# Three small loads moved to the large loads' queue, and the gates computed after q

## The chip, the core and the metric

The kernel runs on one core of one Trainium2 chip. The metric is the time of one execution on the device in microseconds (us). Before the change it was 1347.45 us, the median of three runs (1345.95 to 1347.85).

Engines are called PE (matmuls), PEld (weight loads of PE), DVE (VectorE), ACT (ScalarE), POOL (GpSimd) and SP (SyncE). A "q" behind the name is the engine's sequencer, which issues the transfers and waits on semaphores. A "packet" is one piece of a transfer on one of the core's 16 DMA engines, as the profile records it. A run is called fast here when it took at most 1.5% more than the fastest run of the same kernel.

## The reference

For four sequences of one token each, the kernel mixes an attention block over a cache of 8192 positions with a gated feed-forward block.

```python
g = sigmoid((x * gate_w).sum(-1, keepdims=True))
# a: attention. 4 sequences, 32 heads of 128, 8192 cached positions
q = (x @ wq).reshape(4, 1, 32, 128).transpose(0, 2, 1, 3)
p = softmax(q @ k_cache^T * 128 ** -0.5)
a = (p @ v_cache) ... @ wo
# b: feed-forward, scaled by sigmoid(x @ w_r), plus x   (one token: the argsort picks it)
b = x + ((silu(x @ w_gate) * (x @ w_up)) @ w_down) * sigmoid(x @ w_r)
return g * a + (1 - g) * b
```

Every weight and both caches are read once. The profile counts 575.68 MB of reads, and 93% of that is the two caches (2 x 4 x 32 x 8192 x 128 x 2 bytes = 536.9 MB).

## The kernel before

All large loads go through one ring of five slots in on-chip memory (`ring`, 4 MB each) and through SyncE's queue. A load waits until the slot it overwrites has been read. The first of them, `wq` (8 MB, slots 0 and 1), is hoisted to the very start of the program. A "pair" is 8 MB of the K or of the V cache, in two halves of one slot each. `w_gate` follows in slots 2 and 3, and the first half of K pair 0 in slot 4. The second half of K pair 0 goes into slot 0 again, so it waits for the q matmuls that read the half of `wq` in that slot.

```python
x6 = const.tile([NX, D], BF)             # 4 rows of x, then w_r, then gate_w
nc.scalar.dma_start(out=x6[0:Bn], in_=x2)
nc.scalar.dma_start(out=x6[Bn:Bn + 1], in_=B_w_r.rearrange("(o n) -> o n", o=1))
nc.scalar.dma_start(out=x6[Bn + 1:Bn + 2], in_=gate_w.rearrange("(o n) -> o n", o=1))
... # x6 is transposed on PE and copied to xw
def gates():
    rg_ps = small([P, 2, Bn])
    wrep = ttp.tile([P, 2, DT, P], BF, name="wrep", tag="T")
    for i in range(2):
        nc.vector.tensor_copy(out=wrep[:, i, :, :], in_=xw[:, :, Bn + i:Bn + i + 1].to_broadcast([P, DT, P]))
        for t in range(DT):
            nc.tensor.matmul(rg_ps[:, i, :], lhsT=wrep[:, i, t, :], rhs=xT[t], start=(t == 0), stop=(t == DT - 1))
    nc.scalar.activation(out=sgb[:], in_=rg_ps[:], func=ACT.Sigmoid)
    ...
def wq_piece():
    N = H * Dh
    ws = load_pair(A_wq.rearrange("(c t) n -> c (t n)", t=DT), TW * N)
    x_rows(q_ps, ws, N // NB, lambda w, t, i: w[:, t * N + i * NB:t * N + (i + 1) * NB])
...
gates()
wq_piece()
q_done()
gu_piece(B_w_gate, 0)
... # then 32 pairs of K and of V halves, with w_up, w_down and wo in between
```

PE, DVE and POOL run their instructions in the order of the program.

## Time and profile before

| what | where it is read | value |
|---|---|---|
| time | median of three runs | 1347.45 us |
| bytes moved | DMA part of the page | 576.2 MB, mean 429 GB/s |
| SyncE's queue (q1) | queues, share of 16 engines' span | 99.4% |
| PE, DVE busy | first part of the page | 78%, 46% |
| q matmuls | timeline | 27.1 to 32.9 us |
| first use of w_gate | timeline | 39.85 us |

The lines below are from the page of the kernel before: the busy shares in 40 slices of the span (tenths, 9 is 90% or more), the rate in each slice, the DMA queues (packets, MB, share of 16 engines' span) and the shares of the chain that ended last.

```profile
...
PE   2565877777887778778987789797779679877888
...
DVE  3555655534445554345555446246545254556000
...
DMA  9999999999999999999999999999999999999997
GB/s 414 447 421 428 441 426 428 442 435 422 435 436 426 440 417 431 443 429 434 435 433 431 433 425 431 435 431 438 431 420 438 435 426 432 430 426 438 426 425 327
...
q1 hardware_dynamic: 14120, 575.68, 99.4%
...
q10 hardware_dynamic: 20, 0.02, 0.0%
...
DMA 63%; PE 19%; DVE 11%; issue 7%; another core or an unknown queue 0%; DVEq 0%; ACT 0%; SPq 0%
...
```

The DMA row reads 9 in every slice but the last, and no engine's row does. The chain is mostly DMA too. Queue q10 is ScalarE's: 20 packets, 0.02 MB.

Next is the timeline of the first 62 us (start, duration, engine, line, operation, out<-in, in brackets the idle time before and what ended it). L157 transposes x, L219 is the gates' broadcast copy, L244 holds the matmuls of q (`S_ps`) and of w_gate (`o_ps`).

```profile
...
0.00 0.40 SPq L127 DMA_DIRECT2D ring<-in_A_wq_dram  x1
...
0.80 0.56 ACTq L140 DMA_DIRECT2D x<-in_A_x_dram  x1
...
0.81 0.33 SPq L127 DMA_DIRECT2D ring<-in_B_w_gate_dram  x1
...
1.19 29.92 SPq L131 DMA_DIRECT2D ring<-in_A_k_cache_dram  x2
...
20.20 0.63 PE L157 MATMUL small<-identb,x 6*128 6x6 bf16 x8 [20.20 <-DMA x<-in_gate_w_dram]
...
21.18 5.60 DVE L219 COPY wrep<-xw 128x1024 bf16<-128x1024 bf16 x2
...
27.14 5.73 PE L244 MATMUL S_ps<-ring,xw 128*4 128x512 bf16 x64
...
39.85 6.21 PE L244 MATMUL o_ps<-ring,xw 128*4 128x512 bf16 x56 [3.81 <-DMA ring<-in_B_w_gate_dram]
...
44.33 0.33 SPq L127 DMA_DIRECT2D ring<-in_A_k_cache_dram  x1
...
```

PE stands idle for x until 20.20 us, then waits for the gate copies, and q runs from 27.14 us. But even so it is done before w_gate is there: PE waits another 3.81 us for it.

The third view is SyncE's waits in the first 60 us (line, what for, us in total, times, longest).

```profile
...
SPq L131 <- DMA ring<-in_A_wq_dram: 21.3, 1, 21.3
...
SPq L131 <- PE S_ps L244: 7.9, 1, 7.9
...
```

SyncE waits for the q matmuls once, for 7.9 us, before it can issue the second half of K pair 0.

### The profile page before, as it was taken

What the parts mean: (1) busy time and instruction counts of PE and PEld (TensorE: products, weight loads), DVE (VectorE), ACT (ScalarE), POOL (GpSimd) and SP (SyncE); (2) the same over time, 40 slices, a digit from 0 to 9 for tenths busy, and PEclk for the clock granted to TensorE, in tenths of its full rate; (3) what the DMA queues carried; (4) which work ended last, traced back from release to release, by engine and by line L of the source; (5) the groups of instructions that cost most, each with busy time, mean ns of one, the idle gap of its engine ahead of it and who ended that gap; (6) DMA issues with size and microseconds to landing.
All of it is one profiled execution on the core that took longest, in us unless ns stands there. A gap on an engine that the chain in (4) does not pass through costs nothing.

```text
span 1344.6 us, 7989 instructions
## 1 busy us (share of the span) xinstructions
PE 1050.9 (78%) x4536; PEld 229.7 (17%) x2348; DVE 620.5 (46%) x358; ACT 51.4 (4%) x46; POOL 57.7 (4%) x91
## 2 busy tenths in 40 slices
PE   2565877777887778778987789797779679877888
PEld 0111111112111121111211121111111112111211
DVE  3555655534445554345555446246545254556000
ACT  0000100001000100001000010001000010000000
POOL 3000100001000100001000010000000010000000
PEclk9787988988998889899888889998889898989999
DMA  9999999999999999999999999999999999999997
GB/s 414 447 421 428 441 426 428 442 435 422 435 436 426 440 417 431 443 429 434 435 433 431 433 425 431 435 431 438 431 420 438 435 426 432 430 426 438 426 425 327
DMA packets 14175, 576.20 MB, mean 429 GB/s; under 512 B 1582, under 2 KB 1590, under 8 KB 2108
## 3 DMA queue, kind: packets, MB, share of 16 engines
q1 hardware_dynamic: 14120, 575.68, 99.4%
q8 instruction: 27, 0.44, 0.1%
q14 instruction: 8, 0.07, 0.0%
q10 hardware_dynamic: 20, 0.02, 0.0%
HBM read 575.68 MB, written 0.01 MB: 428 GB/s over the span
## 4 chain that ended last, share of the span: by engine, by line
DMA 63%; PE 19%; DVE 11%; issue 7%; another core or an unknown queue 0%; DVEq 0%; ACT 0%; SPq 0%
DMA ring<-in_A_k_cache_dram 52%; DVE T L370 11%; PE S_ps L376 11%; PE o_ps L447 8%; DMA ring<-in_A_v_cache_dram 7%; DMA ring<-in_B_w_gate_dram 3%; DMA ring<-in_A_wo_dram 1%; PE small L466 1%; DVEq L370 0%; PE acc L210 0%; ACT OS L459 0%; ACT res L513 0%; DVE rinv L420 0%; DVE OS L460 0%
## 5 line engine op out<-in xcount | busy, mean ns | idle before, releaser
L370 DVE STREAM_TRANSPOSE T<-ring 128x2048 uint32<-128x2048 uint32 x256 | 570.5, 2281 | 497.8 <-DMA ring<-in_A_k_cache_dram 416.6
L376 PE MATMUL S_ps<-T,Z 128*128 128x512 bf16 x2048 | 538.3, 411 | 222.3 <-DVE T L370 222.3
L447 PE MATMUL o_ps<-ring,PB 128*32 128x512 bf16 x2048 | 458.0, 386 | 33.4 <-DMA ring<-in_A_v_cache_dram 33.3
L376 PEld LDWEIGHTS <-Z 128*128 128x128 bf16 x1024 | 106.5, 104 | 646.8 <-issue 638.8
L447 PEld LDWEIGHTS <-PB 128*32 128x32 bf16 x1024 | 100.3, 98 | 388.1 <-issue 367.5
L401 ACT ACTIVATE PTs<-S_ps,negm 128x1024 bf16<-128x1024 f32 x8 | 8.9, 1114 | 994.8 <-DVE negm L398 994.8
L353 POOL TENSOR_TENSOR Z<-qa,mq 128x16 bf16<-128x16 bf16 x32 | 8.2, 260 | 809.3 <-PE S_ps L376 734.9
L460 DVE SCALAR_TENSOR_TENSOR OS<-o_ps,mE,OS 128x512 f32<-128x512 f32 x8 | 6.0, 751 | 66.8 <-ACT OS L459 66.8
L412 POOL COPY PB<-PT 32x1024 bf16<-32x1024 bf16 x16 | 30.3, 1892 | 26.8 <-DVE rex L414 26.5
L410 ACT COPY PB<-PT 32x1024 bf16<-32x1024 bf16 x16 | 30.6, 1913 | 10.7 <-DVE PT L403 10.6
L309 DVE CAST LT<-small 128x64 bf16<-128x64 f32 x2 | 0.5, 225 | 46.3 <-PE small L307 46.3
L394 POOL PARTITION_ALL_REDUCE gmx<-mex x8 | 3.2, 394 | 339.0 <-DVE mex L391 339.0
L389 DVE TENSOR_REDUCE m<-S_ps 128x1 f32<-128x1024 f32 x8 | 9.8, 1225 | 15.9 <-PE S_ps L376 15.9
L210 PE MATMUL acc<-ring,LT 128*4 128x512 bf16 x64 | 14.9, 378 | 2.0 <-DMA ring<-in_A_wo_dram 1.2
L157 PE MATMUL small<-identb,x 6*128 6x6 bf16 x8 | 0.6, 196 | 20.2 <-DMA x<-in_gate_w_dram 20.2
L420 DVE RECIPROCAL rinv<-tot 128x16 f32<-128x16 f32 x8 | 2.0, 247 | 31.0 <-POOL tot L416 31.0
L403 DVE STREAM_TRANSPOSE PT<-PTs 128x1024 bf16<-128x1024 bf16 x8 | 10.0, 1246 | 12.1 <-ACT PTs L401 12.1
L466 PEld LDWEIGHTS small<-selg,OS 128*128 128x128 f32 x64 | 12.7, 279 | 6.0 <-issue 5.5
L210 PE MATMUL acc<-ring,hT 128*4 128x512 bf16 x56 | 12.2, 379 | 0.0
L466 PE MATMUL small<-selg,OS 128*128 128x16 f32 x64 | 11.7, 320 | 0.0
L459 ACT ACTIVATE OS<-o_ps,mE 128x512 f32<-128x512 f32 x8 | 5.5, 687 | 118.3 <-PE o_ps L447 118.3
L244 PE MATMUL o_ps<-ring,xw 128*4 128x512 bf16 x56 | 6.2, 573 | 3.8 <-DMA ring<-in_B_w_gate_dram 3.8
(71 smaller groups left out, 88.2 us busy)
## 6 DMA issues: line engine op xcount, KB each, us to landing
ring<-in_A_k_cache_dram SPq DMA_DIRECT2D x14, 4096.0 KB, 33.4
ring<-in_A_v_cache_dram SPq DMA_DIRECT2D x14, 4096.0 KB, 29.6
ring<-in_B_w_gate_dram SPq DMA_DIRECT2D x1, 7168.0 KB, 39.0
ring<-in_B_w_up_dram SPq DMA_DIRECT2D x1, 7168.0 KB
ring<-in_B_w_down_dram SPq DMA_DIRECT2D x2, 3584.0 KB, 25.7
ring<-in_A_wo_dram SPq DMA_DIRECT2D x6, 1024.0 KB, 22.2
ring<-in_A_v_cache_dram SPq DMA_DIRECT2D x2, 2048.0 KB, 31.1
ring<-in_A_v_cache_dram SPq DMA_DIRECT2D x4, 1024.0 KB, 29.0
```

The lines of the kernel that those rows point to most:

```text
L210: nc.tensor.matmul(out_ap, lhsT=lhsT, rhs=rhs, start=start, stop=True, skip_group_check=True)
L244: nc.tensor.matmul(ps[32 * k:32 * k + Bn, z, :], lhsT=xT[TW * half + t], rhs=cols(w, t, 4 * z + k), start=(half + t == 0), stop=(half == 1 ...
L353: nc.gpsimd.tensor_tensor(out=Z[:, :, QP - 1:QP - 1 + P].rearrange("p e (q c) -> p e q c", c=QP)[:, :, :, 0], in0=qa[:, :, h0:h0 + NQ, b], ...
L370: nc.vector.transpose(out=T[:].rearrange("p j h i e -> p (j h i e)").bitcast(U32), in_=kn[:, c * CJ * Dh:(c + 1) * CJ * Dh].bitcast(U32))
L376: nc.tensor.matmul(sps[:, z, :], lhsT=Z[:, he, s:s + P], rhs=T[:, 16 * z:16 * z + 16, half, :, e], start=(t == 0 and n == 0 and he == 0), ...
L389: nc.vector.tensor_reduce(out=m1[:], in_=sps[:].rearrange("p z n -> p (z n)"), axis=AX.X, op=ALU.max)
L401: nc.scalar.activation(out=PTs[:], in_=sps[:].rearrange("p z n -> p (z n)"), func=ACT.Exp, bias=negm[:, 0:1], scale=scale, accum_out=rs[:, ...
L403: nc.vector.transpose(out=PT[:].rearrange("p j i -> p (j i)"), in_=PTs[:])
L410: nc.scalar.copy(out=Bv[at, :, :, q, :], in_=Pv[at])
L412: nc.gpsimd.tensor_copy(out=Bv[at, :, :, q, :], in_=Pv[at])
L447: nc.tensor.matmul(o_ps[row:row + NM, e, :], lhsT=B_[:, RD * t + c, z, w].rearrange("p e s j -> p (e s j)"), rhs=vn[:, j0 * Dh:(j0 + 4) * ...
L466: nc.tensor.matmul(oT[:, :], lhsT=o_sb[:, q * Dh:(q + 1) * Dh], rhs=selg[:, q].rearrange("p t s -> p (t s)"), start=(q == 0), stop=(q == 3))
```

## The change

The intent: the small loads shall stop competing as a second queue with `wq`, and q, which K pair 0's slot waits for, shall come before the gates, which nothing needs early.

```diff
+    N = H * Dh
+    wq_at = load_pair(A_wq.rearrange("(c t) n -> c (t n)", t=DT), DT // 2 * N)
     NX = Bn + 2
     x6 = const.tile([NX, D], BF)
-    nc.scalar.dma_start(out=x6[0:Bn], in_=x2)
-    nc.scalar.dma_start(out=x6[Bn:Bn + 1], in_=B_w_r.rearrange("(o n) -> o n", o=1))
-    nc.scalar.dma_start(out=x6[Bn + 1:Bn + 2], in_=gate_w.rearrange("(o n) -> o n", o=1))
+    nc.sync.dma_start(out=x6[0:Bn], in_=x2)
+    nc.sync.dma_start(out=x6[Bn:Bn + 1], in_=B_w_r.rearrange("(o n) -> o n", o=1))
+    nc.sync.dma_start(out=x6[Bn + 1:Bn + 2], in_=gate_w.rearrange("(o n) -> o n", o=1))
 ...
     def wq_piece():
-        N = H * Dh
-        ws = load_pair(A_wq.rearrange("(c t) n -> c (t n)", t=DT), TW * N)
-        x_rows(q_ps, ws, N // NB, ...)
+        x_rows(q_ps, wq_at, N // NB, ...)
 ...
-    gates()
     wq_piece()
     q_done()
+    gates()
     gu_piece(B_w_gate, 0)
```

More of the change, by code (lines that the diff above doesn't have):

```diff
@@ L247, in wq_piece @@
     def wq_piece():
-        N = H * Dh
-        ws = load_pair(A_wq.rearrange("(c t) n -> c (t n)", t=DT), TW * N)
-        x_rows(q_ps, ws, N // NB, lambda w, t, i: w[:, t * N + i * NB:t * N + (i + 1) * NB])
+        x_rows(q_ps, wq_at, N // NB, lambda w, t, i: w[:, t * N + i * NB:t * N + (i + 1) * NB])
     def q_done():
```

## The prediction

> **What bounds the kernel now.** The transfers. The page shows 576.2 MB at a mean of 429 GB/s; the SyncE queue (q1) is busy 99.4% of 16 engines' span, and every slice but the last reads 9 in the DMA row. PE is busy 78%, DVE 46%. The Trainium skill, page "DMA: Bandwidth & Descriptors", section "Where 436 GB/s comes from", gives 435 GB/s as the fabric's ceiling; the trace's 429 is 98.6% of it, so start, tail and all starved moments together can hardly hold more than 20 us. The tail shows in the timeline: about 6 us after the stream has ended at 1338 us. The change doesn't touch it.
>
> **What the change does.** (a) Three small loads (12 KB) go from ScalarE's queue to SyncE's, behind wq and ahead of w_gate. (b) The gates' two copies on DVE, 16 matmuls and sigmoid go from before the q matmuls to after q is done.
>
> Timeline of before: wq is issued at 0 us and lands at 22.9 us. The small loads, issued by 2.2 us, land only at 20.2 us: their separate queue gave no early arrival (so says the same page, "Issuing engines are not separate DMA queues"). The transposes of x end by 21.0 us, the gate copies run 21.2 to 26.8 us (slow, while GpSimd clears PB), the gate matmuls end at 27.2, the q matmuls run 27.1 to 32.9, q is done at 36.8. The w_gate matmuls wait for their transfer until 39.85 us.
>
> After: x6 lands between 20 and 24 us, q matmuls start at 23 to 25 us (limited by wq's landing) and end near 29 to 31, q is done near 33 to 35, the gates are over by 37. The q stage gains 2 to 4 us. Issuing the small loads on SyncE costs about 1.3 us (0.56, 0.24 and 0.50 us on ScalarE) and delays w_gate's issue from 0.8 to about 2.1 us, with 20 us of wq queued.
>
> **How much is on the critical path.** Almost nothing. The gain ends in the wait for w_gate at 39.85 us. The one issue that q releases is the second half of K pair 0 (31.1 us, after 7.9 us of waiting for the q matmuls); it moves to about 27 us. But by 31.1 us 19.9 MB had been issued and about 12.5 MB moved (estimate: 29 us at 429 GB/s): 17 us of transfers were queued. The next issues (44.3, 58.2, 89.8 us) are released by w_gate matmuls and K transposes, behind the stream; by the same estimate 14, 19 and 5 us were queued there. The queue doesn't run dry before or after.
>
> **Prediction.** 1346.5 us, range 1343 to 1350; faster by over 2%: 0.01, within 2%: 0.98, slower by over 2%: 0.01.
>
> **What would show it.** Right: DMA row 9 throughout at about 429 GB/s; q matmuls about 3 us earlier, gates between q done and w_gate, w_gate matmuls still starting at 39.5 to 40.5 us, K pair 1 still issued at 44 to 45 us, the same tail. In the waits, SyncE's wait for the q matmuls falls from 7.9 to about 4 us. Wrong: x6 landing past 25 us, w_gate's matmuls moving with it, or a slice of the DMA row under 9.
>
> **What would make it wrong.** Small packets in SyncE's rings holding up w_gate or K; a slot freed in another order so that the thin 5 us of queue near 90 us runs dry; a different mean transfer rate from run to run (0.3% is 4 us).

## The result, and the profile after

The changed kernel took 1344.95 us (median of four runs, 1344.77 to 1345.52), beside 1347.65 us of the kernel before (four runs, the three above and one more, 1345.95 to 1349.12). The ratio is 0.9981, with a 95% interval from 0.9964 to 0.9998. A ratio here is the mean time of one kernel's fast runs over that of the other's of the same rounds, so it isn't quite the ratio of the medians. So the change is within 2%, as forecast. The interval stops just short of 1, so the first question is whether the 2.7 us between the medians are real.

These are the same parts of the changed kernel's page.

```profile
...
DMA  9999999999999999999999999999999999999998
GB/s 414 440 427 431 436 430 425 446 427 424 440 430 427 440 433 422 442 434 428 436 434 433 424 431 436 434 434 439 418 424 437 434 429 434 432 429 442 422 425 335
...
q1 hardware_dynamic: 14132, 575.69, 99.5%
...
q10 hardware_dynamic: 8, 0.00, 0.0%
...
DMA 62%; PE 20%; DVE 11%; issue 6%; another core or an unknown queue 0%; DVEq 0%; ACT 0%; SPq 0%
...
```

The rows are those of before: 9 in every slice but the last, and the same rate within the spread of the slices. The 12 packets of the small loads have gone from q10 to q1; the 8 left on q10 are the output's.

This is its timeline (source lines are shifted by two: L159 transposes x, L221 is the gate copy, L246 holds the matmuls of q and w_gate).

```profile
...
0.00 0.39 SPq L127 DMA_DIRECT2D ring<-in_A_wq_dram  x1
...
0.80 0.34 SPq L142 DMA_DIRECT2D x<-in_A_x_dram  x1
...
1.75 0.36 SPq L127 DMA_DIRECT2D ring<-in_B_w_gate_dram  x1
2.15 24.79 SPq L131 DMA_DIRECT2D ring<-in_A_k_cache_dram  x2
...
22.35 0.62 PE L159 MATMUL small<-identb,x 6*128 6x6 bf16 x8 [22.35 <-DMA x<-in_gate_w_dram]
...
23.24 5.04 PE L246 MATMUL S_ps<-ring,xw 128*4 128x512 bf16 x64 [0.27 <-DVE xw L161]
...
32.00 1.35 DVE L221 COPY wrep<-xw 128x1024 bf16<-128x1024 bf16 x2
...
39.00 5.72 PE L246 MATMUL o_ps<-ring,xw 128*4 128x512 bf16 x56 [5.22 <-DMA ring<-in_B_w_gate_dram]
...
43.44 0.33 SPq L127 DMA_DIRECT2D ring<-in_A_k_cache_dram  x1
...
```

The small loads land two microseconds later than before (22.35 against 20.20 us), and yet q starts 3.9 us earlier, because nothing stands between the transposes and q any more. The gate copies take 1.35 us instead of 5.60; they no longer run beside POOL's clearing of the PB tiles, which ended at 24.6 us. That the clearing held them up is read from the times, not from a run of its own: three small DVE instructions just ahead of the copies took 4.5 to 4.7 us in the kernel before and ended within 0.1 us of that clearing (25.6 us), but 0.16 to 0.17 us each in `x_first` (below), where they ran before it. And the gain ends where the prediction said: PE now waits 5.22 us for w_gate instead of 3.81, and starts on it at 39.00 us. K pair 1 is issued at 43.44 us, 0.9 us earlier than before.

SyncE's waits in the first 60 us of the changed kernel:

```profile
...
SPq L131 <- DMA ring<-in_A_wq_dram: 19.3, 1, 19.3
...
SPq L131 <- PE S_ps L246: 4.6, 1, 4.6
...
```

The wait for q shrank from 7.9 to 4.6 us. The wait for `wq`, however, also shrank, from 21.3 to 19.3 us: after SyncE's three extra issues that is a landing of `wq` 0.9 us earlier (22.0 instead of 22.9 us). This was not forecast, and it is what the experiments go after.

### The profile page after: what moved, and what is told of

It is laid out like the page before. It is cut to its first block, busy times and chain, and to the rows that moved or that the text cites. A ratio compares the mean times of both kernels' runs of the same rounds, so it can differ in the third digit from the quotient of the medians.

```text
span 1343.2 us, 7989 instructions
## 1 busy us (share of the span) xinstructions
PE 1050.1 (78%) x4536; PEld 230.3 (17%) x2348; DVE 617.8 (46%) x358; ACT 51.4 (4%) x46; POOL 58.7 (4%) x91
## 3 DMA queue, kind: packets, MB, share of 16 engines
HBM read 575.68 MB, written 0.01 MB: 429 GB/s over the span
## 4 chain that ended last, share of the span: by engine, by line
DMA 62%; PE 20%; DVE 11%; issue 6%; another core or an unknown queue 0%; DVEq 0%; ACT 0%; SPq 0%
DMA ring<-in_A_k_cache_dram 52%; PE S_ps L376 11%; DVE T L370 11%; PE o_ps L447 8%; DMA ring<-in_A_v_cache_dram 7%; DMA ring<-in_B_w_gate_dram 3%; DMA ring<-in_A_wo_dram 1%; PE small L466 1%; DVEq L370 0%; PE acc L212 0%; ACT OS L459 0%; ACT res L513 0%; SPq L142 0%; SPq L144 0%
## 5 line engine op out<-in xcount | busy, mean ns | idle before, releaser
L159 PE MATMUL small<-identb,x 6*128 6x6 bf16 x8 | 0.6, 196 | 22.3 <-DMA x<-in_gate_w_dram 22.3
L246 PE MATMUL o_ps<-ring,xw 128*4 128x512 bf16 x56 | 5.7, 536 | 5.2 <-DMA ring<-in_B_w_gate_dram 5.2
## 6 DMA issues: line engine op xcount, KB each, us to landing
ring<-in_A_v_cache_dram SPq DMA_DIRECT2D x4, 1024.0 KB, 24.6
```

## The experiments

The packets of `wq` tell more than the views above. The median packet of 65,536 bytes took 2.42 us on its engine, in all runs. The first on each engine mostly took about 3 us, and after 9 us another 46 to 88 packets of a run took over 2.62 us, up to 4.5. In the profile of before, however, four packets that started near 6.8 us took 3.05 to 3.49 us, just behind the first four packets of ScalarE's queue on four engines. In the first profile of the changed kernel the slowest packet at that time took 2.68 us. This suggested three theories for the 2.7 us:

- Queue: small packets of a second queue slow four DMA engines by about 1 us each, and since the stream has no slack, that stays until the end.
- Order: q comes earlier, so K pair 0's second half is issued earlier.
- Noise: runs of one kernel differ by as much.

### The two halves of the change, alone

`loads_only` moves the loads and leaves the gates in front. `gates_only` does the opposite.

```diff
 # loads_only, against the changed kernel
+    gates()
     wq_piece()
     q_done()
-    gates()
 # gates_only, against the changed kernel
-    nc.sync.dma_start(out=x6[0:Bn], in_=x2)
+    nc.scalar.dma_start(out=x6[0:Bn], in_=x2)
 ... # and so for the other two
```

> The small loads are moved to SyncE's queue, the gates stay ahead of q. Queue theory (the 1 to 2 us gained come from taking the small packets off ScalarE's queue, where they slowed four DMA engines by about 1.05 us each near 6.8 us): the whole gain of the change, ratio to before 0.998 to 0.9995, wq landing near 22.0 us, no packet of wq near 6.8 us that takes 3.4 us. Order theory (the gain comes from q and K pair 0's second half being issued sooner): q starts later than 25 us again, so the gain is gone, ratio 0.9995 to 1.0005. Noise theory: 1.000 like everything else.

> The small loads stay on ScalarE's queue, the gates come after q. Queue theory: no gain, ratio to before 0.9995 to 1.0005; wq lands near 22.9 us and four packets near 6.8 us take about 3.4 us, although q starts at about 23.5 us. Order theory: the whole gain, ratio 0.998 to 0.9995.

Measured: `loads_only` 1345.37 us, ratio 0.9997 (0.9983 to 1.0011). `gates_only` 1345.38 us, ratio 0.9992 (0.9980 to 1.0004). The kernel before on that chip: 1346.87 us (11 runs). Neither half shows the 0.19%, and the medians, both 1.5 us below, don't tell them apart. But the interval of `gates_only` still holds 0.9981, and its ratio lies in the band that the order theory expected, so this pair alone decides nothing. One run of `loads_only` took 1351.45 us, so single runs stray by several us without any change of clock.

The timelines of `loads_only` and then of `gates_only`: transposes of x, q, w_gate, the issue of K pair 1.

```profile
...
22.52 0.62 PE L159 MATMUL small<-identb,x 6*128 6x6 bf16 x8 [22.52 <-DMA x<-in_gate_w_dram]
...
26.40 5.40 PE L246 MATMUL S_ps<-ring,xw 128*4 128x512 bf16 x64
...
39.11 5.88 PE L246 MATMUL o_ps<-ring,xw 128*4 128x512 bf16 x56 [4.14 <-DMA ring<-in_B_w_gate_dram]
...
43.60 0.33 SPq L127 DMA_DIRECT2D ring<-in_A_k_cache_dram  x1
...
```

```profile
...
19.90 0.63 PE L159 MATMUL small<-identb,x 6*128 6x6 bf16 x8 [19.90 <-DMA x<-in_gate_w_dram]
...
22.93 5.55 PE L246 MATMUL S_ps<-ring,xw 128*4 128x512 bf16 x64 [2.40 <-DMA ring<-in_A_wq_dram]
...
39.88 5.63 PE L246 MATMUL o_ps<-ring,xw 128*4 128x512 bf16 x56 [5.92 <-DMA ring<-in_B_w_gate_dram]
...
44.24 0.33 SPq L127 DMA_DIRECT2D ring<-in_A_k_cache_dram  x1
...
```

The two halves move q as expected: to 26.40 us with the loads alone, to 22.93 us with the order alone (where `wq` itself is what q waits for). The use of w_gate starts at 39.11 and 39.88 us whichever way q goes: with the later q it was even the earlier one. So q's time does not set it.

### q delayed on purpose

`q_late10`, `q_late30` and `q_late60` put 2, 6 and 12 extra passes of the q matmuls, into a bank that w_gate's matmuls overwrite later, in front of the true ones. Results stay right.

```diff
     def wq_piece():
+        for _ in range(2):        # 6, 12
+            x_rows(o_ps, wq_at, N // NB, lambda w, t, i: w[:, t * N + i * NB:t * N + (i + 1) * NB])
         x_rows(q_ps, wq_at, N // NB, ...)
```

> The changed kernel with two extra passes of the q matmuls into a scratch bank ahead of the true ones: q is done about 10 us later (5.0 us a pass). Queue theory, with my estimate of 17 to 21 us of transfers queued at that time: the total stays that of the changed kernel, within 1 us. Order theory: q's time is on the chain, so the total grows by several us, up to 10.

> Six extra passes: q done about 30 us later, so K pair 0's second half is issued near 56 us, while the 19.9 MB issued before it are through at about 48 us (estimate at 430 GB/s). If the queued transfers are the slack, the stream runs dry for about 8 us and the total grows by 8 to 14 us, with a slice of low GB/s near 50 us. If q had no bearing on the stream at all, 0; if q were on the chain throughout, 30.

> Twelve extra passes of the q matmuls; in q_late30 a pass took 3.7 us, so q comes about 44 us late and K pair 0's second half is issued near 70 us, while the transfers issued before it are through at about 48 us. Queued transfers as the slack: beyond some 20 us each further us of q costs a us of the total, so about 20 to 26 us over the changed kernel (1366 to 1372 us), with the transfers idle from about 48 to 71 us. If the small cost of q_late30 came from elsewhere: well under 15 us.

The time of the issue is from the profiled run; the row of the changed kernel is its first result.

| run | second half of K pair 0 issued at, us | median us | ratio to before (95%) |
|---|---|---|---|
| changed | 26.6 | 1344.95 | 0.9981 (0.9964 to 0.9998) |
| q_late10 | 35.4 | 1345.79 | 0.9995 (0.9980 to 1.0009) |
| q_late30 | 47.9 | 1349.11 | 1.0017 (1.0005 to 1.0030) |
| q_late60 | 69.3 | 1369.71 | 1.0168 (1.0152 to 1.0183) |

The timeline of `q_late10`: the two extra passes, q, w_gate, K pair 1.

```profile
...
24.09 9.49 PE L246 MATMUL o_ps<-ring,xw 128*4 128x512 bf16 x128 [0.28 <-DVE xw L161]
...
33.41 3.62 PE L246 MATMUL S_ps<-ring,xw 128*4 128x512 bf16 x64
...
42.45 5.34 PE L246 MATMUL o_ps<-ring,xw 128*4 128x512 bf16 x56
...
46.53 0.33 SPq L127 DMA_DIRECT2D ring<-in_A_k_cache_dram  x1
...
```

Issuing that load 9 us later than in the changed kernel, and 5 us later than before, cost nothing that these runs can show. `q_late30` cost about 2 us beside the kernel before of its call (2.3 by the ratio), or 3 beside `q_late10`, and not the 8 to 14 that I expected, since repeated passes took 3.7 us each instead of 5.0: the load was issued at 47.9 us, just when the 19.9 MB in front of it were through. By the packet records the 16 engines then stood idle for 0.9 us on average. Another 1.2 us were lost near 60 us, because q delayed w_gate's matmuls too, and so the issue of K pair 1, to 59.48 us:

```profile
...
59.48 0.33 SPq L127 DMA_DIRECT2D ring<-in_A_k_cache_dram  x1
...
56.00:60.00 4.00, 4.00 (x39) 0.68 (x20) 4.00 (x2) 0.00 (x0) 0.00 (x0) 0.50 0.61 262
...
```

The second line is a stretch of the kind explained below; its last number is 262 GB/s. Beyond `q_late30` the cost is about one for one: `q_late60` issues it 21 us later still, and takes 20.6 us longer than `q_late30` (the two ran in different calls; the medians of the kernel before beside them were 1346.71 and 1346.87 us).

The stretches of the changed kernel and then of `q_late60` from 48 to 76 us, every other one (columns: stretch, length, busy time and count of PE, PEld, DVE, ACT and POOL, granted clock, DMA share, GB/s).

```profile
...
48.00:52.00 4.00, 0.00 (x0) 0.00 (x0) 1.91 (x1) 0.00 (x0) 0.00 (x0) 0.75 1.02 442
...
56.00:60.00 4.00, 3.80 (x17) 0.77 (x8) 3.94 (x2) 0.00 (x0) 0.00 (x0) 0.89 1.19 516
...
64.00:68.00 4.00, 3.41 (x16) 0.68 (x8) 4.00 (x3) 0.00 (x0) 0.00 (x0) 1.00 1.21 524
...
72.00:76.00 4.00, 0.00 (x0) 0.00 (x0) 0.00 (x0) 0.00 (x0) 0.00 (x0) 0.74 0.98 426
...
```

```profile
...
48.00:52.00 4.00, 4.00 (x80) 0.84 (x36) 0.00 (x0) 0.00 (x0) 0.00 (x0) 1.00 0.06 20
...
56.00:60.00 4.00, 4.00 (x80) 0.88 (x40) 0.00 (x0) 0.00 (x0) 0.00 (x0) 1.00 0.01 4
...
64.00:68.00 4.00, 4.00 (x80) 0.84 (x36) 0.00 (x0) 0.00 (x0) 0.00 (x0) 1.00 0.02 4
...
72.00:76.00 4.00, 1.52 (x20) 1.02 (x20) 2.56 (x6) 0.00 (x0) 1.02 (x2) 1.00 1.06 459
...
```

In `q_late60` nothing moves between about 50 and 70 us, and it resumes when q lets it. In the changed kernel the same stretches are full. Summed over 44 to 100 us, an engine's mean idle time is 23.2 us in `q_late60`, 2.1 us in `q_late30` and under 0.1 us in `q_late10`, the changed kernel and the one before. That is the time lost (about 22.6 and 2.3 us by the ratios). The slack can also be counted directly: when the kernel before issues that load (30.8 us), 12.4 of the 19.9 MB have moved, and the rest is 17 us of transfers at 2.42 us a packet. In the changed kernel (26.6 us) it is 21 us, and the change only moves q within it. The order theory is refuted.

### The same kernels again

`after_a` and `after_b` are the changed kernel, `before_a` and `before_b` the one before, all unchanged, on one chip.

> The changed kernel once more, unchanged. If the 0.19% of the first result is real, the ratio to before is 0.998 to 0.999 again; if it is noise, 0.9995 to 1.0005. Since q_late10, which has no load on ScalarE's queue, also had four slow packets near 6.8 us, I now expect such packets to come and go between runs whatever the queue, and the gain to be below 0.1%.

> The kernel before against itself: the ratio must be 1.000, and its distance from 1 and its interval give the noise floor. Queue theory: four packets of 3.4 us near 6.8 us again. Noise: they are of another size.

> A third time the changed kernel, for its spread: same expectation as for after_a. Queue theory: the slow packets near 6.8 us stay under 0.4 us of excess. Noise: some run shows about 1 us.

> A second control of the kernel before against itself: ratio 1.000; differences between before_a and before_b as large as those between either and after_a mean that 0.1% can't be told apart here.

| run | median us | range | ratio to the runs of before (95%) |
|---|---|---|---|
| after_a | 1346.00 | 1344.99 to 1346.14 | 1.0001 (0.9988 to 1.0013) |
| after_b | 1347.04 | 1344.88 to 1348.57 | 1.0007 (0.9995 to 1.0020) |
| before_a | 1345.77 | 1344.72 to 1346.20 | 0.9999 (0.9985 to 1.0012) |
| before_b | 1346.65 | 1345.42 to 1347.02 | 1.0004 (0.9992 to 1.0017) |
| before, reference | 1345.45 | 1344.97 to 1348.22 | |

On this chip the 10 runs of the changed kernel have a mean of 1346.24 us and the 19 runs of the kernel before 1345.98 us. The difference is 0.27 us, with a standard error of 0.40 us worked out from the spread of single runs (1.1 and 0.9 us). The 0.19% of the first result did not come back, and the intervals of both repeats leave it out. Which chip gave that first result is not on record, so a gain on that chip alone isn't excluded. The medians of two sets of five runs of one and the same kernel differ by 0.9 and 1.0 us here.

### Small packets on the second queue, added

`act3` is the changed kernel with three more loads of four rows each on ScalarE's queue at the start, into a tile that nobody reads.

```diff
     gates()
     gu_piece(B_w_gate, 0)
+    spare = const.tile([P, 448], BF, name="spare")
+    for i in range(3):
+        nc.scalar.dma_start(out=spare[Bn * i:Bn * i + Bn], in_=x2[:, 0:448])
```

> The changed kernel with three more four-row loads on ScalarE's queue at the start, into a spare tile, so as many or more small packets on that queue as in the kernel before (24 against 12). Queue theory: four DMA engines lose about 1 us each near 6.8 us and the total grows by about 1 us; Noise: slow packets of 0.2 to 1.1 us as in all runs, total within 1 us of the changed kernel's.

Measured: 1346.36 us, ratio 0.9994 (0.9979 to 1.0009). No cost shows. (The edit also moved SyncE's issue of K pair 0's first half from 2.15 to 9.80 us, with `wq` and w_gate queued in front.) The four slowest packets of 65,536 bytes that start between 6.3 and 9 us, from the packet records of every profile, show how much of this goes with the queue:

```
run          packets on ScalarE's queue   slowest four packets there, us
before        12                          3.49 3.48 3.43 3.05
before_a      12                          2.91 2.91 2.91 2.89
before_b      12                          3.13 3.08 3.07 2.73
gates_only    12                          3.62 3.10 3.06 2.60
act3          24                          2.89 2.71 2.65 2.43
changed        0                          2.68 2.58 2.46 2.42
after_a        0                          2.71 2.63 2.63 2.52
after_b        0                          2.97 2.90 2.88 2.76
loads_only     0                          2.79 2.74 2.69 2.42
q_late10       0                          3.54 3.46 3.46 3.38
q_late30       0                          3.05 2.91 2.72 2.47
q_late60       0                          2.93 2.89 2.82 2.65
x_first        0                          2.43 2.42 2.42 2.42
```

`q_late10`, with nothing on ScalarE's queue, has four packets as slow as those of the kernel before, and `act3`, with twice the packets there, has not. What slows a few packets near 6.8 us, by anything from 0.2 to 1.2 us, is not the small loads alone; whether they add a few tenths on average can't be told from so few profiles. What it is stays open. It is also where `wq`'s earlier landing in the first pair of profiles came from: its last large packet ended at 22.49 us in the kernel before and 21.59 us in the changed one, but at 22.36 us in `q_late10`, with no small load on ScalarE's queue and packets as slow as before.

### x before everything

`x_first` puts the three small loads on SyncE's queue ahead of `wq`, so x comes as early as it can, and the first large transfer starts later.

```diff
-    wq_at = load_pair(A_wq.rearrange("(c t) n -> c (t n)", t=DT), DT // 2 * N)
     NX = Bn + 2
     ... # x6 and its three loads on nc.sync
+    wq_at = load_pair(A_wq.rearrange("(c t) n -> c (t n)", t=DT), DT // 2 * N)
```

> The three small loads on SyncE's queue ahead of wq: x is there within a few us, but wq, the first large transfer, is issued at about 1.5 us instead of 0. If the start of the stream sets the end, the total is 1 to 2 us longer than the changed kernel's although x is there some 15 us earlier; if the arrival of x mattered, it would be shorter. Either is within the noise of single runs (about 1 us), so the timeline decides: first packet of wq near 2.5 us instead of 1.0 us, and the last weights landing as much later.

Its timeline: the issues of x and `wq`, the transposes of x, q.

```profile
...
0.00 0.37 SPq L141 DMA_DIRECT2D x<-in_A_x_dram  x1
...
1.38 0.36 SPq L127 DMA_DIRECT2D ring<-in_A_wq_dram  x1
...
10.04 0.60 PE L159 MATMUL small<-identb,x 6*128 6x6 bf16 x8 [10.04 <-DVE identb L156]
...
23.52 6.48 PE L246 MATMUL S_ps<-ring,xw 128*4 128x512 bf16 x64 [12.88 <-DMA ring<-in_A_wq_dram]
...
```

x is transposed at 10.04 us, 12 us earlier than in the changed kernel, and q still starts at 23.52 us, because then it waits for `wq`. The first packet of `wq` starts at 2.36 us instead of 1.02, and the last large packet of the stream ends at 1340.56 us, where the three profiles of the changed kernel have 1338.80, 1340.02 and 1339.57 us. That goes the way of a later start, but its size lies within the spread. The time, 1346.92 us with a ratio of 0.9999 (0.9982 to 1.0015), can't decide it: inconclusive for the 1.3 us, clear in that an early x does not bring q forward.

No version beats both kernels. All of them read the same 575.68 MB, and at 65,536 bytes per 2.42 us on 16 engines that alone is about 1329 us (an estimate from these numbers).

## Why the prediction was right

- "The transfers" bound the kernel: right. Three kernels with q at 23, 27 and 33 us have the same time within the noise, and the only kernels that lost time, `q_late30` and `q_late60`, are those that let the transfers run dry.
- x6 between 20 and 24 us, the q matmuls from 23 to 25 us: right (22.35 and 23.24 us). But "limited by wq's landing" was wrong in the changed kernel: `wq` had landed at 22.0 us, and q waited for x, its transposes and the copy behind it. (In `gates_only` and `x_first`, where x came earlier, q did wait for `wq`.)
- q done near 33 to 35 us: slightly too late. The matmuls ended at 28.3 us, ahead of the 29 to 31 forecast, since they took 5.04 us instead of the 5.73 us of before, and the last copy of q ended at 32.1 us. Gates over by 37: right (34.5 us).
- "17 us of transfers were queued": right, and now shown by the delays: up to 9 us of delay were free, 21 us beyond that slack cost 20.6 us. At the next three issues the packet records of before give 13.5, 19.0 and 4.3 us queued, where the prediction had 14, 19 and 5. The thin place near 90 us held with 3.4 us in the changed kernel; no run stretched it.
- Issuing the small loads on SyncE delayed w_gate's issue by 0.9 us (1.75 us) and not 1.3. The same tail: right, 4.4 us after the last large packet in both; the "about 6 us" read it too long.
- w_gate's matmuls at 39.5 to 40.5 us and K pair 1 at 44 to 45 us: 39.00 and 43.44 us, both half a microsecond outside. The step that failed was to take one trace for the value: three profiles of the kernel before have 39.85, 39.23 and 39.43 us, and 44.33, 42.91 and 43.92 us.
- SyncE's wait for q from 7.9 to about 4 us: right (4.6 us).
- The time, 1346.5 us in 1343 to 1350, same by 0.98: right. The first result alone would have suggested a gain of 0.19%; the repeats gave 1.0001 and 1.0007, so no gain is shown. "Same" was a weak test, since a few us either way stay within 2%; the delays are the strong one.

Three sections of one page bear on the argument. The Trainium skill, page "DMA: Bandwidth & Descriptors", section "Where 436 GB/s comes from", gives 435 GB/s as a ceiling; the trace agrees with 429 GB/s over the whole span. The same page's section "Issuing engines are not separate DMA queues" says that loads from different engines share the same 16 DMA engines and interleave; the packets of the kernel before show just how. On the engine that carries all three small loads, the order was this (start, queue, bytes, duration in us, from the packet records):

```
  4.35 q1  65536 2.42
  6.76 q10  2048 0.08     x
  6.84 q1  65536 3.05
  9.89 q10     4 0.01     x done (this engine's part)
  9.89 q1  65536 2.42
 12.31 q10  2048 0.08     w_r
 12.39 q1  65536 2.42
 14.80 q10     4 0.01     w_r done
 14.81 q1  65536 2.42
 17.22 q10  2048 0.08     gate_w
 17.30 q1  65536 2.42
 19.72 q10     4 0.01     gate_w done
```

Its section "Queues, rings and completion order" says that an engine takes turns between queues packet by packet. The trace agrees. A packet there is typically 9 to 17 descriptors (single moves), while here every record took a turn of its own: each small packet after the first, and each 4-byte completion too, waits for one packet of 65,536 bytes of the other queue. So each small load took two turns, mostly of 2.42 us, and three in a row landed at 19.7 us. The first small packet came only at 6.76 us, behind two large packets, though it was issued by 1.4 us; why not behind one stays open. Behind `wq` in the same queue they land when `wq` does, which is 2 us later. The separate queue was worth 2 us to the loads, so "no early arrival" in the prediction was slightly too strong, and neither choice was worth anything to the kernel.

## What to carry to other kernels

If a kernel is bound by one stream of transfers that never runs dry, work in front of an issue is free as long as it fits in what is queued ahead: count the bytes issued and not yet moved at that time before moving anything, and at the issues behind it too (`q_late30` lost more at the next one). A gain near 0.2% whose interval barely misses 1 has to be repeated against a control of the same kernel. Here a small load on a second queue beside large row transfers waited one large packet for its data and one for its completion (2.42 us each), so several in a row add up; making them one load was not tried.

## What the Trainium skill lacked or had wrong

- "DMA: Bandwidth & Descriptors", section "Specifications", gives about 27 GiB/s per engine. The packets show 65,536 bytes in 2.42 us, which is 27.1 GB/s (25.2 GiB/s); 16 times that is 433 GB/s, in line with the same page's 435 GB/s.
- The same page, section "Where 436 GB/s comes from", says that about 358 GB/s of HBM bandwidth per core bind loads from HBM, without the condition that its table of measurements has, that both cores of a pair stream. With one core running, this kernel loaded 575.68 MB from HBM at 428 GB/s over its span, which agrees with the 425 GB/s that the page itself measured for one core.
- The same page, section "Queues, rings and completion order", doesn't say what a turn costs a small load beside long rows. Here a turn was one packet of 65,536 bytes, 2.42 us, and a load of 2,048 bytes took two turns because its 4-byte completion waited as well, in a turn apart from its data.
- No page that I read has an explanation for the few packets near 6.8 us that took 0.2 to 1.2 us longer than 2.42 us in 12 of 13 profiles, nor for the 46 to 88 later ones that took over 2.62 us.
- No page that I read gives the spread of one kernel's runs: here 0.9 to 1.1 us of standard deviation (0.07 to 0.08%), with one stray run of 1351.45 us.
